# Attention, LayerNorm and feed-forward on one core: four weight halves ahead of the units, an earlier LayerNorm row, and one load for each tail bias tile

## The chip, the core and the metric

The kernel runs on one core of one Trainium2 chip. The metric is the device time of one execution in microseconds (us), taken as the median of the runs shown. Five engines matter: TensorE (PE, with its weight loads as PEld), VectorE (DVE), ScalarE (ACT), GpSimd (POOL) and SyncE (SP). SP and POOL issue nearly all of the DMA transfers.

## What is computed

There are 4 batches of 8 heads, a sequence of 576 and a head width of 64. The feed-forward part goes from 512 to 2048 and back to 512 columns.

```python
scores = scale * np.matmul(q, k.transpose(0, 1, 3, 2))
x = (psi_rel / psi_i)[..., None]
bias = np.maximum(x @ w1 + b1, 0.0) @ w2          # per head, 576 x 576
scores = scores + bias.transpose(2, 0, 1)[None]
attn = softmax(scores)                             # over the last axis
x = matmul(attn, v)                                # heads joined to 512
xn = (x - mean) / np.sqrt(var + 1e-06) * g_ln
out = x + np.maximum(xn @ w_ch1, 0.0) @ w_ch2
```

## The kernel before

**Bias.** The bias is the same for all batches, so it is built once. Its 36 groups of 16 rows go through a small network on ACT, DVE and PE (`bias_relu` L153, `bias_mm` L167). `bias_mm` evicts a group to a staging tile `ev` and writes that by DMA to a DRAM tensor `nb`, of which there is one for each chunk `c` of 128 rows (chunk 4, the tail, has only 64). The first 12 groups are written by POOL's queue, the rest by SP's. The order of the groups begins with the tail chunk: its four groups are needed first.

**Units.** The attention is cut into 144 units (b, c, h), a batch, a chunk of rows and a head; a tail unit (c = 4) holds two heads of 64 rows each. The list `ORD` (L213) sets their order: (0, 4), (1, 4), (1, 0), (0, 0), ... Each unit takes four score matmuls (`qk` L377, written to `sps`), one DVE instruction that adds the bias tile `ldb` and takes the row maximum (L434 in `softmax1`, called "softmax u" below), an exp on ACT (L438), and the product with V (`pv` L496, written to `xps`). The first 24 units keep their probabilities in f32 and are transposed on PE (`ptm` and `ptl`); later ones are cast to f16 and transposed by DMA.

**Bias tiles and other loads.** `issue_loads(u)` (L277) issues the loads of K, Q and V on POOL's queue and those of bias tiles on SP's, as their due times in units come. A tail bias tile is read in two loads of 64 rows (L328, L329).

**Weights.** The two feed-forward matrices arrive as 32 halves of 512 KB, each on SP's queue (`load_w` L610, the load on L627). While `n < 24` a load that is issued inside the loop over units waits for the latest softmax. `decode_w` (L634) turns a half into f32 by three DVE instructions (L643, L646, L648) and feeds a Gram matmul on PE (L657). When the last half of a group (0 to 4, 4 to 8, 8 to 16 of the 16 row blocks) is decoded, `w_scale` (L660) derives the group's scales (`winv`, `wred`), and `split_w` (L677) makes an f16 high part on ACT (L683) and a low part on DVE (L686).

**The loop.** Two halves are loaded and decoded ahead of the loop (L812, L828). Step `u` runs softmax 1 of unit `u`, the loads that are due, two `load_w` calls, and as many decodes as the pace asks for:

```python
if wdec and 32 - len(wdec) < 2 + (4 * max(0, u - 1) + 2) // 3:
```

The row `gs_sb` (LayerNorm's g) is loaded in step 1 behind a wait for the latest softmax (L846); `g_scale` (L692, first instruction L693) reads it in step 3. In step 9, `FILL` (L403) puts 68 matmuls without use (`spin`, L410) on PE. Feed-forward work is cut into micros that fill PE between units: `hps` (L709) is the first product, `y` (L738) the second, with evictions on ACT (L715) and DVE (L719, L749). A scheduler sets the order of instructions on each engine from priorities and dependencies, and each engine executes in that order.

Of the kernel before, what the change touches and what calls it, by code (L numbers as in the profile page):

```python
# [22 lines left out]
def kernel(  # L23
# [14 lines left out]
    NB, NH, SEQ, D = 4, 8, 576, 64  # L38
# [23 lines left out]
    def halves(t):  # L62
# [29 lines left out]
        for c in range(5)  # L92
    ]
    nbias = [
        t[0:(128 if c < 4 else 64) * NH * PITCH].rearrange("(i h j) -> i h j", h=NH, j=PITCH)
        [:, :, 16:16 + SEQ] for c, t in enumerate(nflat)
    ]
    wslot = [wp.tile([128, 1024], F32, name=f"w{f}") for f in range(NF - 1)]
    wend = wp.tile([128, 2048], F32, name="wend")
    wslot += [wend[:, 0:1024], wend[:, 1024:2048]]  # L100
# [37 lines left out]
    def after(ins, dep):  # L138
        if dep is not None:
            tc.add_manual_dep(ins.ins, dep.ins.name,  # L140
                              mybir.DependencyInfo(mybir.DependencyClass.Sync,
                                                   mybir.DependencyReason.DATA),
                              reason="pace")
# [23 lines left out]
    def bias_mm(gi):  # L167
# [40 lines left out]
        dst = nflat[c][r0 * row:(r0 + 16) * row + 16]  # L208
        dst = dst.rearrange("(k x) -> k x", k=16)[:, 0:row]
        dst = dst.rearrange("k (h j) -> k h j", h=NH)[:, :, 0:ntot]  # L210
        (G if gi in gorder[0:12] else SY).dma_start(out=dst, in_=ev[:, 0:ntot])

    ORD = [(0, 4), (1, 4), (1, 0), (0, 0), (2, 0), (3, 0), (3, 4), (2, 4),  # L213
# [20 lines left out]
    uv = {}  # L234
# [29 lines left out]
    for u, (b, c, h) in enumerate(units):  # L264
        key = (seg[vis[u]], c, h)
        buse[key] = buse.get(key, 0) + 1
    vneed = {0: -5, 1: 1, 2: min(uv[2] - 15, ustart[2, 0] - 8),
             3: min(uv[3] - 15, ustart[3, 0] - 8)}
    for b in range(NB):
        for g in range(4):  # L270
# [6 lines left out]
    def issue_loads(u):  # L277
        wait = set()
        for item in list(loads):
# [31 lines left out]
            elif kind == "v":  # L311
                raw = vp.tile([128, 640], F32, tag="v", name="vf")
                ld = G.dma_start(out=raw.rearrange("p (a b c) -> p a b c", a=2, b=5),
                                 in_=v_p[key[0], :, 2 * key[1]:2 * key[1] + 2])
                if ttri:
                    after(ld, ttri[max(ttri)])
                vraw[key] = raw
            else:
                _, c, h = key
                if not bfree[0] or mm_done[0] < gend[c]:  # L320
                    wait.add(kind)
                    continue
                bfree[0] -= 1
                raw = ldp.tile([128, SEQ], F32, tag="ld", name="ldb")
                if c < 4:
                    SY.dma_start(out=raw, in_=nbias[c][:, h, :])
                else:
                    SY.dma_start(out=raw[0:64], in_=nbias[4][:, 2 * h, :])  # L328
                    SY.dma_start(out=raw[64:128], in_=nbias[4][:, 2 * h + 1, :])  # L329
                bt[key] = raw  # L330
            loads.remove(item)

# [476 lines left out]
    wload = [(f, i) for f in range(NF) for i in range(2)]  # L809
    wdec = list(wload)  # L810
    NP = 7
    for _ in range(2):  # L812
        load_w()
    issue_loads(-6)
    issue_loads(-5)
# [5 lines left out]
    for n in range(NP + 1):  # L821
        if n < NP:
            bias_relu(gorder[n], 3)
        if n > 0:
            bias_mm(gorder[n - 1])
            mm_done[0] += 1
    ngroup = NP
    for _ in range(2):  # L828
        decode_w(*wdec.pop(0))

    def flush():
# [6 lines left out]
    def at(step, fn):  # L838
        todo.setdefault(step, []).append(fn)

    for b in range(NB):
        u0 = uv[b]
        for g in range(4):
            at(u0 - 11 + g, lambda b=b, g=g: v_max(b, g))
            at(u0 - 4 + 2 * g if b else u0 - 4 + 2 * g, lambda b=b, g=g: split_v(b, g))
    at(1, lambda: after(SY.dma_start(out=gs_sb, in_=g_r), ttri[max(ttri)]))  # L846
    at(3, g_scale)
    issue_loads(0)
    qk(0)
    qk(1)  # L850
    with tc.high_priority(offset=-40):
# [12 lines left out]
    while u < NU + 6 or jobs or cur_job or pend or yq:  # L864
# [16 lines left out]
            if wload:  # L881
                load_w()
        for _ in range(8):
            if wdec and 32 - len(wdec) < 2 + (4 * max(0, u - 1) + 2) // 3:
                f, i = wdec.pop(0)
                decode_w(f, i)
                if i == 1 and f + 1 == GROUPS[GOF[f]][1]:
                    w_scale(GOF[f])
# [106 lines left out]
```

## Time and profile before

| what | us |
| --- | --- |
| three runs | 678.59, 682.61, 681.12 |
| median | 681.12 |
| span of the profiled execution | 676.2 |
| busy PE / DVE / ACT / POOL in it | 647.0 / 457.6 / 392.0 / 97.3 |

The profiled execution's own time is not listed apart from its span; the span is 4.9 us under the median of the runs (681.12 - 676.2). A busy time is the sum over instructions of one engine. The notation `[2.81 <-DMA gs_sb<-in_g_r_dram]` at a row's end says how long the engine stood idle just before the row, and what ended that. An engine name with a q (SPq) is its sequencer: the time for which it issues a transfer.

### The profile page before, as it was taken

Reading aid. Unit: us, or ns where it says so; the run is one execution under the profiler, and the core shown is the slowest. Engines: PE = TensorE matmul, PEld = TensorE weight load, DVE = VectorE, ACT = ScalarE, POOL = GpSimd, SP = SyncE. Lnnn points to the kernel's source line nnn. Section 1 sums busy time; section 2 is a strip of 40 time slices with the busy share of each in tenths; the row PEclk is TensorE's granted clock in tenths of the full one; section 3 lists DMA queues with packets and bytes.
Section 4 is the critical chain, followed back from the end, with each engine's and each line's share of the span. In section 5 each row is a group of like instructions: output and inputs, shape, how many; then the busy total and the mean of one; then the engine's idle time right before and its main releaser. Section 6 shows DMA issues by size and latency. Waiting matters only on the chain.

```text
span 676.2 us, 19145 instructions
## 1 busy us (share of the span) xinstructions
PE 647.0 (96%) x7929; PEld 448.4 (66%) x7929; DVE 457.6 (68%) x1061; ACT 392.0 (58%) x777; POOL 97.3 (14%) x163
## 2 busy tenths in 40 slices
PE   6789996999999999999899999999999999999997
PEld 4457774676466666666667766666776776677774
DVE  6588999679757577696757575667576675755321
ACT  5565747378958466887755576676554454453110
POOL 5412321011000011111101010111011120000000
PEclk9989997899999999999899999999999999999999
DMA  8999885444668997868769779699997886744100
GB/s 313 295 405 335 298 291 173 143 87 105 136 132 169 227 235 171 176 154 169 174 159 223 156 161 174 151 182 180 184 214 150 160 162 121 128 88 87 33 16 17
DMA packets 187015, 117.24 MB, mean 173 GB/s; under 512 B 164016, under 2 KB 164144, under 8 KB 186928
## 3 DMA queue, kind: packets, MB, share of 16 engines
q1 hardware_dynamic: 177184, 81.00, 54.7%
q0 software_dynamic: 9600, 34.84, 17.0%
q8 instruction: 62, 1.02, 0.6%
q10 hardware_dynamic: 144, 0.18, 0.1%
q14 instruction: 25, 0.20, 0.1%
HBM read 60.51 MB, written 15.63 MB: 113 GB/s over the span
## 4 chain that ended last, share of the span: by engine, by line
PE 50%; DVE 0%; ACT 0%; issue 0%
PE hps L709 19%; PE y L738 18%; PE sps L391 6%; PE xps L480 6%; PE bps L181 1%; DVE v L369 0%; DVE x L749 0%; DVE e L462 0%; ACT e L443 0%; DVE x L516 0%; ACT t L438 0%; DVE e L464 0%
## 5 line engine op out<-in xcount | busy, mean ns | idle before, releaser
L709 PE MATMUL hps<-xT,w 128*128 128x128 f16 x3240 | 197.1, 221 | 2.8 <-DVE w L686 2.1
L738 PE MATMUL y<-w,hh 128*128 128x512 f16 x810 | 189.8, 382 | 2.9 <-ACT hh L715 2.8
L709 PEld LDWEIGHTS <-w 128*128 128x128 f16 x3240 | 185.4, 99 | 8.3 <-DVE w L686 3.6
L438 ACT ACTIVATE t<-t,m 128x576 f32<-128x576 f32 x144 | 110.9, 770 | 135.6 <-DVE m L434 135.2
L738 PEld LDWEIGHTS <-hh 128*128 128x128 f16 x864 | 79.8, 98 | 91.9 <-ACT hh L715 3.9
L462 DVE SCALAR_TENSOR_TENSOR e<-t,e 128x512 f16<-128x512 f32 x120 | 82.8, 690 | 77.1 <-ACT e L443 76.8
L434 DVE CUSTOM_DVE_ANT_0 t<-sps,ldb 128x576 f32<-128x576 f32 x144 | 105.9, 753 | 33.7 <-PE sps L391 20.8
L391 PE MATMUL sps<-kf,qf 64*128 64x288 f32 (+1 forms) x640 | 95.9, 434 | 4.3 <-DVE m L434 4.3
L443 ACT ACTIVATE e<-t 128x576 f16<-128x576 f32 x120 | 80.8, 678 | 4.9 <-DMA wend<-e 2.5
L715 ACT ACTIVATE hh<-hps 128x512 f16<-128x512 f32 x72 | 42.0, 583 | 52.4 <-PE hps L709 46.9
L391 PEld LDWEIGHTS sps<-kf,qf 64*128 64x128 f32 (+1 forms) x640 | 48.0, 175 | 36.6 <-issue 17.5
L719 DVE SCALAR_TENSOR_TENSOR hh<-hps,hh 128x512 f16<-128x512 f32 x72 | 49.4, 686 | 33.2 <-ACT hh L715 32.7
L480 PEld LDWEIGHTS <-pt 128*128 128x128 f16 (+1 forms) x1456 | 48.9, 100 | 30.0 <-issue 25.6
L749 DVE SCALAR_TENSOR_TENSOR x<-y,ycs,x 128x512 f32<-128x512 f32 x58 | 43.4, 748 | 34.5 <-PE y L738 34.4
L480 PE MATMUL xps<-v,pt 128*128 128x64 f16 (+1 forms) x1456 | 58.6, 194 | 1.5 <-DMA pt<-e 1.1
L291 POOL DMA_DIRECT2D kf<-in_k_s_dram x56 | 30.8, 551 | 162.0 <-PE sps L391 114.6
L304 POOL DMA_DIRECT2D qf<-in_q_main_dram x32 | 18.4, 576 | 159.8 <-PE xps L480 81.5
L187 ACT ACTIVATE ev<-bps,cb_sb,par_sb 128x144 f32<-128x144 f32 (+27 forms) x48 | 26.0, 592 | 25.8 <-PE bps L181 25.7
L160 ACT ACTIVATE r<-psi_sb,par_sb 128x448 f32<-128x448 f32 (+23 forms) x72 | 39.6, 613 | 0.0
L569 POOL TENSOR_SCALAR rs<-mv 128x1 f32<-128x1 f32 x18 | 9.9, 548 | 146.2 <-DVE mv L568 138.3
L438 ACT ACTIVATION_READ_ACCUMULATOR t<-t,m 128x1 f32 x144 | 27.0, 188 | 0.0
L181 PE MATMUL bps<-r,nw_sb 128*32 128x448 f32 (+24 forms) x200 | 26.9, 494 | 0.0
(121 smaller groups left out, 642.8 us busy)
## 6 DMA issues: line engine op xcount, KB each, us to landing
kf<-in_k_s_dram POOLq DMA_DIRECT2D x56, 288.0 KB, 4.9
w<-in_w_ch_dram SPq DMA_DIRECT2D x22, 512.0 KB, 8.4
ldb<-nb SPq DMA_DIRECT2D x32, 288.0 KB, 4.4
qf<-in_q_main_dram POOLq DMA_DIRECT2D x32, 256.0 KB, 4.7
nb<-ev SPq DMA_DIRECT2D x24, 296.0 KB, 3.3
vf<-in_v_p_dram POOLq DMA_DIRECT2D x16, 320.0 KB, 7.4
wend<-in_w_ch_dram SPq DMA_DIRECT2D x8, 512.0 KB, 4.8
out_dram<-x SPq DMA_DIRECT2D x16, 256.0 KB, 2.3
```

The costliest lines, as they stand in the source:

```text
L160: S.activation(r[:, 0:n], psi_sb[:, 0:n], AF.Relu, bias=pr_sb[:, g4:g4 + 1], scale=1.0)
L391: m = T.matmul(out=o, lhsT=l, rhs=kk, start=True, stop=True, tile_position=(64 * hf, 64 * e))
L434: ttri[u] = V.tensor_tensor_reduce(out=halves(t), in0=ps[:, :, 0:HS], in1=halves(bias), scale=-0.125, scalar=3e38, op0=ALU.add, op1=ALU.mi ...
L438: S.activation(t, t, AF.Exp, bias=m, scale=-1.0, accum_out=l8[b, c][:, h:h + 1])
L443: S.activation(e16[:, 0:SEQ], t, AF.Copy, scale=E_SCALE)
L462: V.scalar_tensor_tensor(out=e16[:, 640:1152], in0=t[:, 0:512], scalar=E_SCALE, in1=e16[:, 0:512], op0=ALU.mult, op1=ALU.subtract)
L480: T.matmul(out=o, lhsT=p[:, m], rhs=v[:, j, a, :], start=(i == 0), stop=(i == len(ops) - 1))
L709: T.matmul(out=h[:, idx * n:idx * n + n], lhsT=w[:, wo + kk * 128:wo + kk * 128 + 128], rhs=xT[k][:, xo + kk, 0:n], start=(i == 0), stop=( ...
L715: S.activation(hh[:, 0], h, AF.Relu)
L719: V.scalar_tensor_tensor(out=hh[:, 1], in0=h, scalar=0.0, in1=hh[:, 0], op0=ALU.max, op1=ALU.subtract)
L738: T.matmul(out=yps[k][t], lhsT=hh[:, a, o:o + 128], rhs=w[:, wo:wo + 512], start=(f == f0 and i == 0), stop=(f == f1 - 1 and i == 2))
L749: V.scalar_tensor_tensor(out=x, in0=y, scalar=ycs[:, g:g + 1], in1=x, op0=ALU.mult, op1=ALU.add)
```

## The change

Five edits. Four halves instead of two are loaded and decoded ahead of the loop, the pace starts from 4, and a half is decoded only if its load has been issued. The load of `gs_sb` stands ahead of the first `qk` and waits for nothing. The V tiles of batch 0 are due from step -3 instead of -5, and `issue_loads(-3)` is called once inside the bias prologue. The tail chunk's `nb` is laid out by head and row, so that a unit's tile is one block of 128 rows, read by one load. Lines after the edits are 3 to 5 higher.

```diff
--- before.py
+++ after.py
@@ -92,9 +92,10 @@
         for c in range(5)
     ]
     nbias = [
-        t[0:(128 if c < 4 else 64) * NH * PITCH].rearrange("(i h j) -> i h j", h=NH, j=PITCH)
-        [:, :, 16:16 + SEQ] for c, t in enumerate(nflat)
+        t[0:128 * NH * PITCH].rearrange("(i h j) -> i h j", h=NH, j=PITCH)[:, :, 16:16 + SEQ]
+        for t in nflat[0:4]
     ]
+    nbias.append(nflat[4][0:64 * NH * PITCH].rearrange("(x j) -> x j", j=PITCH)[:, 16:16 + SEQ])
     wslot = [wp.tile([128, 1024], F32, name=f"w{f}") for f in range(NF - 1)]
     wend = wp.tile([128, 2048], F32, name="wend")
     wslot += [wend[:, 0:1024], wend[:, 1024:2048]]
@@ -208,6 +209,9 @@
         dst = nflat[c][r0 * row:(r0 + 16) * row + 16]
         dst = dst.rearrange("(k x) -> k x", k=16)[:, 0:row]
         dst = dst.rearrange("k (h j) -> k h j", h=NH)[:, :, 0:ntot]
+        if c == 4:
+            dst = nflat[4][r0 * PITCH:r0 * PITCH + 1]
+            dst = bass.AP(dst.tensor, dst.offset, [[PITCH + 1, 16], [64 * PITCH, NH], [1, ntot]])
         (G if gi in gorder[0:12] else SY).dma_start(out=dst, in_=ev[:, 0:ntot])
 
     ORD = [(0, 4), (1, 4), (1, 0), (0, 0), (2, 0), (3, 0), (3, 4), (2, 4),
@@ -264,7 +268,7 @@
     for u, (b, c, h) in enumerate(units):
         key = (seg[vis[u]], c, h)
         buse[key] = buse.get(key, 0) + 1
-    vneed = {0: -5, 1: 1, 2: min(uv[2] - 15, ustart[2, 0] - 8),
+    vneed = {0: -3, 1: 1, 2: min(uv[2] - 15, ustart[2, 0] - 8),
              3: min(uv[3] - 15, ustart[3, 0] - 8)}
     for b in range(NB):
         for g in range(4):
@@ -325,8 +329,7 @@
                 if c < 4:
                     SY.dma_start(out=raw, in_=nbias[c][:, h, :])
                 else:
-                    SY.dma_start(out=raw[0:64], in_=nbias[4][:, 2 * h, :])
-                    SY.dma_start(out=raw[64:128], in_=nbias[4][:, 2 * h + 1, :])
+                    SY.dma_start(out=raw, in_=nbias[4][128 * h:128 * h + 128, :])
                 bt[key] = raw
             loads.remove(item)
 
@@ -809,7 +812,7 @@
     wload = [(f, i) for f in range(NF) for i in range(2)]
     wdec = list(wload)
     NP = 7
-    for _ in range(2):
+    for _ in range(4):
         load_w()
     issue_loads(-6)
     issue_loads(-5)
@@ -824,8 +827,10 @@
         if n > 0:
             bias_mm(gorder[n - 1])
             mm_done[0] += 1
+        if n == 5:
+            issue_loads(-3)
     ngroup = NP
-    for _ in range(2):
+    for _ in range(4):
         decode_w(*wdec.pop(0))
 
     def flush():
@@ -843,9 +848,9 @@
         for g in range(4):
             at(u0 - 11 + g, lambda b=b, g=g: v_max(b, g))
             at(u0 - 4 + 2 * g if b else u0 - 4 + 2 * g, lambda b=b, g=g: split_v(b, g))
-    at(1, lambda: after(SY.dma_start(out=gs_sb, in_=g_r), ttri[max(ttri)]))
     at(3, g_scale)
     issue_loads(0)
+    SY.dma_start(out=gs_sb, in_=g_r)
     qk(0)
     qk(1)
     with tc.high_priority(offset=-40):
@@ -881,7 +886,7 @@
             if wload:
                 load_w()
         for _ in range(8):
-            if wdec and 32 - len(wdec) < 2 + (4 * max(0, u - 1) + 2) // 3:
+            if wdec and wdec[0] in wraw and 32 - len(wdec) < 4 + (4 * max(0, u - 1) + 2) // 3:
                 f, i = wdec.pop(0)
                 decode_w(f, i)
                 if i == 1 and f + 1 == GROUPS[GOF[f]][1]:
```

On SP, at the start of the program, before (the `w` tiles are raw weight halves, `ldb` a bias tile, `nb` its DRAM tensor):

```order
L328 DMA ldb<-nb_128 64x576
L329 DMA ldb<-nb_128 64x576
L627 DMA w_129<-in_w_ch_dram 128x1024
L627 DMA w_132<-in_w_ch_dram 128x1024
L627 DMA w_133<-in_w_ch_dram 128x1024
L627 DMA w_134<-in_w_ch_dram 128x1024
L846 DMA gs_sb<-in_g_r_dram 128x512
L627 DMA w_135<-in_w_ch_dram 128x1024
```

The change, from the first weight load on:

```order
L630 DMA w_129<-in_w_ch_dram 128x1024
L630 DMA w_131<-in_w_ch_dram 128x1024
L630 DMA w_132<-in_w_ch_dram 128x1024
L630 DMA w_133<-in_w_ch_dram 128x1024
L853 DMA gs_sb<-in_g_r_dram 128x512
L332 DMA ldb<-nb_128 128x576 x4
L630 DMA w_129<-in_w_ch_dram 128x1024
L630 DMA w_133<-in_w_ch_dram 128x1024
```

Two weight loads and that of `gs_sb` now stand ahead of the tail bias tiles; a tile is one row instead of two; `gs_sb` no longer stands among the loads that wait for a softmax.

On DVE, around the first softmax (L434 before, L437 now; the row with `m` reads out its maximum), before:

```order
L648 SCALAR_TENSOR_TENSOR w_130<-w_129,w_130 128x512
L648 SCALAR_TENSOR_TENSOR w_130<-w_131,w_130 128x512
L434 ISA t,m<-sps,ldb 128x576
L434 ISA m 128x1
L434 ISA t,m<-sps,ldb 128x576
L434 ISA m 128x1
L162 TENSOR_SCALAR rh<-psi_sb,npr_sb 128x512 x2
L434 ISA t,m<-sps,ldb 128x576
L434 ISA m 128x1
L643 TENSOR_SCALAR w_131<-w_129 128x512
```

The change:

```order
L651 SCALAR_TENSOR_TENSOR w_130<-w_129,w_130 128x512
L651 SCALAR_TENSOR_TENSOR w_130<-w_131,w_130 128x512
L646 TENSOR_SCALAR w_131<-w_132 128x512
L646 TENSOR_SCALAR w_131<-w_133 128x512
L649 SCALAR_TENSOR_TENSOR w_131<-w_132,w_131 128x512
L649 SCALAR_TENSOR_TENSOR w_131<-w_133,w_131 128x512
L651 SCALAR_TENSOR_TENSOR w_131<-w_132,w_131 128x512
L651 SCALAR_TENSOR_TENSOR w_131<-w_133,w_131 128x512
L437 ISA t,m<-sps,ldb 128x576
L437 ISA m 128x1
L437 ISA t,m<-sps,ldb 128x576
L437 ISA m 128x1
```

The six instructions that decode halves 2 and 3 have moved from behind the third softmax to ahead of the first.

On DVE again, around softmax 21 (the `ISA` row; L686, now L689, are the low parts of the splits of weight group 1), before:

```order
L686 SCALAR_TENSOR_TENSOR w_134<-w_135,ws,w_134 128x512
L369 SCALAR_TENSOR_TENSOR v<-vf,vs,v 128x10x64
L646 SCALAR_TENSOR_TENSOR w_142<-w_143,w_142 128x512
L577 SCALAR_TENSOR_TENSOR u<-x,mv,gs_sb 128x512
L434 ISA t,m<-sps,ldb 128x576
L434 ISA m 128x1
L686 SCALAR_TENSOR_TENSOR w_134<-w_135,ws,w_134 128x512
L686 SCALAR_TENSOR_TENSOR w_135<-w_136,ws,w_135 128x512
L648 SCALAR_TENSOR_TENSOR w_142<-w_143,w_142 128x512
L369 SCALAR_TENSOR_TENSOR v<-vf,vs,v 128x10x64
L599 SCALAR_TENSOR_TENSOR x_1639<-u,rs,x_1639 128x512
```

The change:

```order
L689 SCALAR_TENSOR_TENSOR w_135<-w_136,ws,w_135 128x512
L649 SCALAR_TENSOR_TENSOR w_143<-wend,w_143 128x512
L689 SCALAR_TENSOR_TENSOR w_136<-w_137,ws,w_136 128x512
L651 SCALAR_TENSOR_TENSOR w_143<-wend,w_143 128x512
L105 TENSOR_SCALAR vs<-var 128x4
L571 BN_AGGR mv<-bs 128x2
L651 SCALAR_TENSOR_TENSOR w_143<-wend,w_143 128x512
L689 SCALAR_TENSOR_TENSOR w_136<-w_137,ws,w_136 128x512
L359 TENSOR_SCALAR c_1472<-vs 128x8
L580 SCALAR_TENSOR_TENSOR u<-x,mv,gs_sb 128x512
L437 ISA t,m<-sps,ldb 128x576
L437 ISA m 128x1
```

All eight splits of group 1 now stand ahead of softmax 21; before, three did, four stood between softmax 21 and softmax 22, and the last behind softmax 22. On POOL's queue the first K, Q and V loads stand in the order that they had.

## Rows read from the trace of the kernel before

**Rows 1.** Page: busy time of PE, and its busy tenths in 40 slices.

```profile
PE 647.0 (96%) x7929; PEld 448.4 (66%) x7929; DVE 457.6 (68%) x1061; ACT 392.0 (58%) x777; POOL 97.3 (14%) x163
...
PE   6789996999999999999899999999999999999997
```

**Rows 2.** Page: the chain that ended last, by line of the kernel.

```profile
PE hps L709 19%; PE y L738 18%; PE sps L391 6%; PE xps L480 6%; PE bps L181 1%; DVE v L369 0%; DVE x L749 0%; DVE e L462 0%; ACT e L443 0%; DVE x L516 0%; ACT t L438 0%; DVE e L464 0%
```

**Rows 3.** Windows of 15 us: window and length, busy us (instructions) by engine, clock, DMA, GB/s.

```profile
90.00:105.00 15.00, 15.00 (x158) 12.07 (x158) 14.86 (x37) 6.76 (x15) 3.21 (x6) 1.00 0.82 286
105.00:120.00 15.00, 8.46 (x62) 4.96 (x60) 15.00 (x31) 10.96 (x20) 2.76 (x4) 0.68 0.35 98
120.00:135.00 15.00, 14.65 (x95) 10.25 (x96) 9.92 (x23) 5.28 (x14) 0.54 (x1) 0.86 0.50 161
...
150.00:165.00 15.00, 13.44 (x168) 8.56 (x169) 14.00 (x30) 13.17 (x24) 3.24 (x5) 1.00 0.37 81
165.00:180.00 15.00, 14.08 (x138) 8.39 (x138) 13.00 (x27) 15.00 (x29) 0.11 (x1) 1.00 0.62 125
```

**Rows 4.** Timeline of DVE, 20 to 68 us: start, busy us, instruction, idle time before it.

```profile
23.36 0.76 DVE L434 CUSTOM_DVE_ANT_0 t<-sps,ldb 128x576 f32<-128x576 f32 x1 [2.74 <-DMA ldb<-nb]
...
27.24 0.76 DVE L434 CUSTOM_DVE_ANT_0 t<-sps,ldb 128x576 f32<-128x576 f32 x1 [3.12 <-PE bps L201]
...
31.05 0.43 DVE L643 TENSOR_SCALAR w<-w 128x512 uint32<-128x512 uint32 x1 [1.43 <-DMA w<-in_w_ch_dram]
...
40.16 0.69 DVE L693 TENSOR_REDUCE gmax<-gs_sb 128x1 f32<-128x512 f32 x1 [2.81 <-DMA gs_sb<-in_g_r_dram]
...
58.95 0.16 DVE L668 TENSOR_SCALAR wred<-gram 128x2 f32<-128x2 f32 x1 [2.24 <-PE gram L132]
...
67.58 0.76 DVE L434 CUSTOM_DVE_ANT_0 t<-sps,ldb 128x576 f32<-128x576 f32 x1
```

**Rows 5.** Groups by line on DVE: the decoding instructions, busy us and mean ns.

```profile
L646 DVE SCALAR_TENSOR_TENSOR w<-w,w 128x512 uint32<-128x512 uint32 x22 | 14.8, 685 | 0.1
...
L643 DVE TENSOR_SCALAR w<-w 128x512 uint32<-128x512 uint32 x22 | 9.0, 423 | 1.5 <-DMA w<-in_w_ch_dram 1.4
```

**Rows 6.** Windows of 2 us early on, same columns as Rows 3.

```profile
4.00:6.00 2.00, 0.28 (x8) 0.20 (x8) 1.48 (x5) 1.46 (x2) 1.78 (x4) 1.00 1.01 416
...
16.00:18.00 2.00, 1.93 (x41) 1.24 (x32) 2.00 (x6) 1.89 (x3) 0.81 (x2) 1.00 0.65 182
```

**Rows 7.** Transfers issued by SP up to 62 us: count, KB each, median us to landing.

```profile
w<-in_w_ch_dram SPq DMA_DIRECT2D x15, 512.0 KB, 7.8
...
ldb<-nb SPq DMA_DIRECT2D x9, 144.0 KB, 5.9
...
gs_sb<-in_g_r_dram SPq DMA_DIRECT2D x1, 256.0 KB, 11.1
```

**Rows 8.** Timeline of SP's sequencer, 18 to 30 us.

```profile
18.52 0.55 SPq L328 DMA_DIRECT2D ldb<-nb  x1
...
24.15 4.86 SPq L627 DMA_DIRECT2D w<-in_w_ch_dram  x4
```

**Rows 9.** Timeline of PE, 68 us: the first scores behind the spins.

```profile
68.40 0.76 PE L391 MATMUL sps<-kf,qf 64*128 64x288 f32 x4 [0.62 <-DVE m L434]
```

**Rows 10.** Timeline of DVE: softmax 21 and the last split of group 1.

```profile
109.80 0.74 DVE L434 CUSTOM_DVE_ANT_0 t<-sps,ldb 128x576 f32<-128x576 f32 x1
...
118.54 0.74 DVE L686 SCALAR_TENSOR_TENSOR w<-w,ws,w 128x512 f16<-128x512 f32 x1
```

**Rows 11.** Timeline of PE, 116 to 125 us.

```profile
116.00 0.73 PE L709 MATMUL hps<-xT,w 128*128 128x128 f16 x10 [2.15 <-DVE w L686]
...
118.77 1.03 PE L738 MATMUL y<-w,hh 128*128 128x512 f16 x2 [1.35 <-ACT hh L715]
...
121.35 3.72 PE L738 MATMUL y<-w,hh 128*128 128x512 f16 x10
```

**Rows 12.** The chain of waits late in the program: start, us, and twelve `y` matmuls.

```profile
528.80 2.59 PE y L738 x12
```

## The prediction

> **What bounds the kernel now.** I read the page first. PE is busy 96% of the span, and in the 40 slices its digit is 9 nearly everywhere but in the first three, in slice 7, in slice 20 and in the last [rows 1]. The chain that ended last is feed-forward and attention matmuls, with the lines of DVE and ACT at 0% each [rows 2]. So the late part is PE back to back, and a change in loads and weight decoding can only act where PE is not full: before about 185 us. Next I read windows of 15 us over that stretch [rows 3]. Between 105 and 120 us PE works 8.46 of 15 us, DVE all 15.00: there DVE is the bound, and the granted clock is 0.68, so that part of the stretch ran at the lower of PE's two levels (1.2 and 2.4 GHz). From 150 to 180 us ACT is nearly full (13.17 and 15.00 of 15). What DVE does at 105 us it could not do before, so the third view is DVE's own timeline, for idle time ahead of that. From 19 to 59 us it stands idle five times at length: 2.74 us ahead of softmax 0, 3.12 ahead of softmax 1, 1.43 for the third weight half, 2.81 for `gs_sb`, 2.24 for a matmul of the scales of group 0 [rows 4]. These make 12.3 us. From 90 to 120 us DVE is busy 29.86 of 30 us [rows 3]. So the argument is: an idle microsecond of DVE that is filled early is one less of DVE work in the stretch where PE waits for it.
>
> **The two extra halves.** A half costs DVE three instructions, 423, 685 and about 685 ns [rows 5], 1.8 us, so two cost 3.6. They move, they are not added: all 32 halves are decoded in both. They now stand behind the second half's decode, which ends at 20.6 us (23.36 less the 2.74 of idle time), and ahead of softmax 0, that is, in the first hole. With them DVE is ready for softmax 0 at about 24.1, against 23.36 now. If the bias tile still lands when it does, the first hole is gone and softmax 0 is 0.8 us later.
>
> **What the earlier loads cost.** Two halves and `gs_sb` are 1.31 MB more in front of the K, Q, V loads and the writes of the tail bias. Between 4 and 6 us the DMA engines move 416 GB/s at a share of 1.01; between 16 and 18 us 182 GB/s at 0.65 [rows 6]. At 416 GB/s the 1.31 MB last 3.2 us. The slack of the second window is (416 - 182) GB/s times 2 us, 0.47 MB or 1.1 us, and there is more next to it. So softmax 0 is held up by something between nothing and 3.2 us: between 24.1 and 26.5 us. I take 24.8, because the weight halves are needed only at 20 us while the slack lies ahead of that; 0.7 us of the first hole stays. The rule that speaks against this edit is that of the Trainium skill, page "DMA: Bandwidth & Descriptors", section "Issuing engines are not separate DMA queues": transfers that different engines start run on the same 16 DMA engines and interleave. By that rule the whole 3.2 us would fall on POOL's transfers, and the sum below would be the second rival's; the trace agrees in so far as the share is already 1.01 with both queues at work.
>
> **One load for a tail tile.** SP issued the eight half tiles from 18.52 us on, 0.55 us for the first [rows 8], some 4.4 us in all; four whole ones take 2.2 us. The tile of unit 1 is then issued at about 19.1 and, with a landing of 5.9 us as of the half tiles [rows 7], is there at about 25.0, when softmax 0 is just done. The second hole goes from 3.12 to nothing, but unit 2 then waits some 0.7 us for its scores, since PE was not ahead there; I keep 0.7, bounds 0 and 3.1. The four tail tiles later in the program save 2.2 us of SP's time, which no row waits for: nothing. The write to `nb` has as many pieces of the same size: nothing.
>
> **The fifth half.** Its load waits for softmax 0, as that of the third half did. That one was issued 0.8 us behind softmax 0 [rows 4, 8] and its data came about 7 us later. With softmax 0 at 24.8 the fifth half is there at 25.6 plus 6.8, or plus the median of 7.8 [rows 7], at 32.4 to 33.4; DVE has by then done softmax 2 and what follows and stands there at about 30.1. The hole of 1.43 becomes 2.2 to 3.3; I take 2.8. The waiting instruction holds the units behind it too, as it did before. The condition that a half's load must have been issued only moves a decode in the order.
>
> **`gs_sb` and the scales.** The row is issued about 28 us earlier, needs at most its landing time of 11.1 us [rows 7], and is there long before step 3: 2.81 goes to nothing. The scales of group 0 come a unit earlier, with decodes beside them; the hole of 2.24 is between 0 and 2.24 and I take 1.2. The V tiles of batch 0 stand on POOL's queue where they stood: nothing.
>
> **The sum.** Of 12.3 us of holes 0.7 + 0.7 + 2.8 + 1.2 = 5.4 stay, so DVE gains 6.9. By the order, and with each instruction at its group's mean, the work on DVE ahead of softmax 8 is 49.9 us, against 46.8 before: softmax 8 comes at 67.58 [rows 4] + 3.1 - 6.9 = 63.8, and 3.1 us of later decoding are done by then. The 68 spins and the scores behind them, which waited for DVE [rows 9], follow 3.8 us earlier. Until softmax 21 the work ahead of it is 96.5 us against 90.2, with all splits of group 1 in it; the last one of these came at 118.54 [rows 10]. It moves from behind about 119 us of the timeline to about 106 to 108, so `hps` does not wait the 2.15 us that stand ahead of it at 116, nor `y` the 1.35 [rows 11]. Where DVE is the bound, its 6.9 us pass on whole.
> To this comes the clock. Ten `y` took 3.72 us at 121 us [rows 11], while twelve take 2.59 late in the program [rows 12], 2.16 for ten. A full clock in the two windows from 105 to 135 would be worth (1 - 0.68) x 8.46 + (1 - 0.86) x 14.65 = 4.8 us at most, nothing at least; I take half, 2.4, since PE is not idle so often but still idle. Against it, from 150 to 180 us ACT sets the pace; PE stands idle 1.56 + 0.92 = 2.5 us there [rows 3], and with PE earlier it waits more: between 0 and 2.5, I take 1.4. The sum is -6.9 - 2.4 + 1.4 = -7.9 us. The profiled execution has a span of 676.2, so 668.3 after; the median of the runs is 4.9 above that span, and I add it: **673.2 us**.
>
> **The rivals.**
> *PE is full anyway (0.17).* From 68.40 us on, behind a wait of 0.62, PE works, and in the window from 90 to 105 it is at 15.00 of 15 [rows 3, 9]. If the stretch behind does not shorten, because the same splits and decodes meet the same units a little earlier, what is left is the earlier arrival, 3.8 us: 677.3. For it: the DVE work between softmax 20 and 21 grows. Against it: PE's idle time at 116 to 119 has splits and evictions behind it as its releasers.
> *The loads collide (0.18).* The 3.2 us fall on the bias writes whole. Softmax 0 comes at 26.5, the holes that stay are 2.4 + 0.7 + 2.8 + 1.2 = 7.1, DVE gains 5.2, the clock half of what I took: -5.2 - 1.2 + 1.4 = -5.0, or 676.1. For it: the share of 1.01. It decides from a softmax 0 beyond about 25.5.
> *The pile ahead of softmax 21 (0.13), slower.* Between softmax 20 and 21 DVE has 15.4 us of work instead of 10.9, and all of it is executed in order. The units behind have nothing to give PE meanwhile. PE stands idle 4.5 us more, a further stretch like that from 105 to 120 at the lower clock costs 2.7, and the 3.3 us of work that now stand ahead of softmax 31 fall into the window in which ACT and DVE are nearly full. With the 3.8 of earlier arrival: 4.5 + 2.7 + 3.3 - 3.8 = +6.7, or 687.8. It decides if softmax 21 comes later than 112, against 109.80 now [rows 10]. Against it: the feed-forward work of group 0, and of group 1 as soon as its splits are done, lies ready for PE.
> *The change doesn't do what it says (0.10).* The wait for the third half is replaced by a like wait for the fifth and the holes ahead of softmax 0 and 1 come back in other places; only the 2.81 of `gs_sb` remain: 678.3.
>
> **How the numbers follow.** The forecast has 0.42. A measurement of this kernel can tell about 0.5%, 3.4 us, from no change: below 677.7 is faster, above 684.5 slower. Faster is the forecast, most of the second rival (0.15) and half of the first (0.09): 0.66. Same is the rest of these and most of the last: 0.20. Slower is the third and a remnant: 0.14. The lower end has every hole but that of the fifth half (2.2) closed and the clock full, 10.1 + 4.8 = 14.9 less: 666.2, which I round to 666.5. The upper end takes in all rivals but the third: 681.0.
>
> **What would show it.** Right: softmax 0 at 24 to 25.5, no idle time ahead of the maximum of `gs_sb`, a hole of 2 to 3.5 us ahead of the fifth half, softmax 8 at about 63.8, the last split of group 1 by 108, PE over 10 of 15 us between 105 and 120. Wrong: softmax 0 beyond 25.5 (loads collide); softmax 8 early but PE's idle time moved and as long (PE full); softmax 21 beyond 112 (pile); a hole of 5 us or more anywhere before 60 us.

## The result, and the profile after

The changed kernel takes 670.23 us, the median of 4 runs (669.15 to 672.57), against 679.86 (677.76 to 682.61) for the kernel before: a ratio of 0.9863, with a 95% interval of 0.9827 to 0.9899. The forecast was 673.2. On another occasion (e5 below) the ratio was 0.9848 (0.9801 to 0.9895). Some runs of a kernel are over 1.5% slower than its fastest, mostly at a lower granted clock: ratios leave these out, the medians given here do not.

The span of the profiled execution is 668.3 us, against 676.2. That is 7.9 less, which is what the sum of the prediction came to; how much of that is luck is said further down. The execution itself took 670.07, so 1.8 us lie around its span; the prediction had added 4.9, the distance of the old span from the old median, and that is why its time is 3 us too long.

First the windows of 15 us of the changed kernel, with the columns of [rows 3]:

```profile
90.00:105.00 15.00, 13.28 (x120) 10.00 (x120) 13.77 (x33) 7.47 (x14) 1.75 (x4) 0.88 0.68 249
105.00:120.00 15.00, 13.38 (x104) 10.07 (x103) 13.04 (x26) 8.76 (x20) 2.92 (x4) 0.89 0.58 124
120.00:135.00 15.00, 14.36 (x139) 11.80 (x139) 12.38 (x35) 11.28 (x27) 2.37 (x4) 1.00 0.43 118
...
150.00:165.00 15.00, 12.82 (x164) 8.08 (x160) 13.44 (x28) 14.47 (x27) 2.80 (x4) 1.00 0.55 118
165.00:180.00 15.00, 15.00 (x146) 7.90 (x145) 9.31 (x22) 10.00 (x20) 0.00 (x0) 1.00 0.55 102
```

PE is busy 13.38 of 15 us between 105 and 120, where it was 8.46, and the granted clock there is 0.89 instead of 0.68. The window before it has become worse: 13.28 at a clock of 0.88, where it was 15.00. DVE is no longer full in either. So a low clock and idle time have moved ahead and have shrunk.

The same can be had for the whole span, by adding up windows of 2 us: PE's idle time is their length less PE's busy time, and the clock's loss is busy time times (1 - granted clock). What is left is PE's work at full clock.

| stretch, us | idle before | idle after | clock's loss before | clock's loss after |
| --- | --- | --- | --- | --- |
| 0 to 60 | 12.2 | 12.0 | 1.6 | 0.0 |
| 60 to 105 | 1.1 | 2.0 | 0.0 | 2.0 |
| 105 to 135 | 6.5 | 2.3 | 5.3 | 1.2 |
| 135 to 185 | 2.5 | 3.0 | 0.0 | 0.0 |
| from 185 | 6.8 | 8.4 | 1.7 | 0.0 |
| sum | 29.2 | 27.7 | 8.6 | 3.1 |

The work left is 638.5 and 637.4. Of 7.9 us the clock's loss makes 5.5 and idle time 1.5, and 8.3 of all of it is in the stretch from 105 to 135. PE's idle time ahead of 60 us, where the prediction closes holes of DVE, is the same as before (12.0 against 12.2).

Now DVE's timeline, with the rows that answer to [rows 4] (softmax is on L437 in the changed file, decoding begins on L646):

```profile
26.47 0.76 DVE L437 CUSTOM_DVE_ANT_0 t<-sps,ldb 128x576 f32<-128x576 f32 x1 [2.66 <-DMA ldb<-nb]
...
29.91 0.76 DVE L437 CUSTOM_DVE_ANT_0 t<-sps,ldb 128x576 f32<-128x576 f32 x1 [0.48 <-PE sps L394]
...
31.11 0.43 DVE L646 TENSOR_SCALAR w<-w 128x512 uint32<-128x512 uint32 x1 [0.43 <-DMA w<-in_w_ch_dram]
...
33.22 0.43 DVE L646 TENSOR_SCALAR w<-w 128x512 uint32<-128x512 uint32 x1 [0.95 <-DMA w<-in_w_ch_dram]
...
36.86 0.67 DVE L696 TENSOR_REDUCE gmax<-gs_sb 128x1 f32<-128x512 f32 x1
...
54.61 0.14 DVE L671 TENSOR_SCALAR wred<-gram 128x2 f32<-128x2 f32 x1
...
64.25 0.76 DVE L437 CUSTOM_DVE_ANT_0 t<-sps,ldb 128x576 f32<-128x576 f32 x1
```

Softmax 0 comes at 26.47 and not at 23.36, with 2.66 us of idle time still ahead of it, although 3.5 us of decoding have been put in. Softmax 1 follows without a gap, softmax 2 waits 0.48 us for its scores, the fifth and sixth halves 0.43 and 0.95. The maximum of `gs_sb` at 36.86 and `wred` at 54.61 wait for nothing, though the load of `gs_sb` took 14.0 us to land, more than the 11.1 that the prediction called the most. All idle time between the decoding and softmax 8 that a row of the timeline names (2.66, 0.58, 0.48, 0.43, 0.95, 0.75, 0.30, 0.21 and 0.35) is 6.7 us, against 12.5 before. Softmax 8 is 3.3 us earlier.

Why softmax 0 is late is in the transfers that POOL issued in the first 20 us: count, KB each, and the median us from issue to landing. The kernel before:

```profile
nb<-ev POOLq DMA_DIRECT2D x6, 296.0 KB, 3.5
vf<-in_v_p_dram POOLq DMA_DIRECT2D x4, 320.0 KB, 7.4
```

The changed kernel:

```profile
nb<-ev POOLq DMA_DIRECT2D x6, 296.0 KB, 7.7
vf<-in_v_p_dram POOLq DMA_DIRECT2D x4, 320.0 KB, 11.8
```

The writes of the bias and the V tiles take over 4 us longer to land. SP's own queue shows what follows from it:

```profile
22.53 2.56 SPq L332 DMA_DIRECT2D ldb<-nb  x4
27.26 9.90 SPq L630 DMA_DIRECT2D w<-in_w_ch_dram  x8
```

The tail tiles are issued at 22.53, not 18.52 [rows 8], as their writes have landed only then (the first four took a median of 8.5 us, before 3.4). This agrees with the rule that the prediction took from the Trainium skill, page "DMA: Bandwidth & Descriptors", section "Issuing engines are not separate DMA queues".

### The profile page after: what moved, and what is told of

It reads as the page before. It is cut to its first block, busy times and chain, and to the rows that moved or that the text cites. A ratio compares the mean times of both kernels' runs of the same rounds, so it can differ in the third digit from the quotient of the medians.

```text
span 668.3 us, 19124 instructions
## 1 busy us (share of the span) xinstructions
PE 640.6 (96%) x7929; PEld 447.0 (67%) x7929; DVE 456.5 (68%) x1061; ACT 391.5 (59%) x777; POOL 95.7 (14%) x163
## 5 line engine op out<-in xcount | busy, mean ns | idle before, releaser
L741 PE MATMUL y<-w,hh 128*128 128x512 f16 x810 | 187.7, 379 | 3.6 <-DVE x L752 1.6
L437 DVE CUSTOM_DVE_ANT_0 t<-sps,ldb 128x576 f32<-128x576 f32 x144 | 105.7, 752 | 30.7 <-PE sps L394 18.1
L483 PEld LDWEIGHTS <-pt 128*128 128x128 f16 (+1 forms) x1456 | 48.6, 100 | 29.2 <-issue 24.1
```

Of the source, the lines that this page charges most:

```text
L437: ttri[u] = V.tensor_tensor_reduce(out=halves(t), in0=ps[:, :, 0:HS], in1=halves(bias), scale=-0.125, scalar=3e38, op0=ALU.add, op1=ALU.mi ...
L483: T.matmul(out=o, lhsT=p[:, m], rhs=v[:, j, a, :], start=(i == 0), stop=(i == len(ops) - 1))
L741: T.matmul(out=yps[k][t], lhsT=hh[:, a, o:o + 128], rhs=w[:, wo:wo + 512], start=(f == f0 and i == 0), stop=(f == f1 - 1 and i == 2))
```

## The experiments

The comparisons with the kernel before are each with its runs beside them on the same chip; e1 to e4, e5 to e8 and e9 to e12 were run together, and the kernel before had medians of 682.07, 684.16 and 681.11 us there. In the edits, `...` marks what is left out. The edits are against the changed kernel unless said otherwise. Theory A is the prediction's: DVE's early idle time is what counts, and its parts add up. The rivals are named where they came up. The landmark "softmax 36" is used in a table at the end.

**e1: `gs_sb` late again.**

```diff
+    at(1, lambda: after(SY.dma_start(out=gs_sb, in_=g_r), ttri[max(ttri)]))
     at(3, g_scale)
     issue_loads(0)
-    SY.dma_start(out=gs_sb, in_=g_r)
```

> The change, but gs_sb is loaded where it was before (step 1, behind a softmax and the weight loads). Theory A (DVE's early idle time is what counts): a hole of 2 to 3 us ahead of gmax comes back, softmax 8 is 2 to 3 us later than in the changed kernel (64.3), the time is 2 to 3 us longer, about 672.7. Theory B (what counts is that the splits of group 1 stand ahead of softmax 21, which they do here too): softmax 8 is later, but the time stays within 1 us of 670.2.

Measured: 675.79 us, ratio 0.9896 (0.9834 to 0.9957). The hole is back, in DVE's timeline of this kernel:

```profile
41.74 0.69 DVE L696 TENSOR_REDUCE gmax<-gs_sb 128x1 f32<-128x512 f32 x1 [3.55 <-DMA gs_sb<-in_g_r_dram]
```

Softmax 8 comes at 66.93, 2.7 us later than in the change, as A says. By the ratios the time is 3.3 us longer than the change has in e5 (0.9896 against 0.9848, times 682), with intervals that overlap, so that the size of this loss is not settled. The profiled execution, which was the slowest of the six, shows something else. Two windows of it, columns as above:

```profile
66.00:77.00 11.00, 9.05 (x77) 6.38 (x75) 10.91 (x25) 4.88 (x13) 3.29 (x5) 1.00 0.82 266
77.50:101.50 24.00, 24.00 (x114) 19.31 (x113) 21.33 (x53) 13.46 (x33) 4.61 (x8) 0.50 0.79 284
```

PE was busy 9.05 of 11 us from 66 to 77, then the granted clock is 0.50, the lower of the two levels, for 24 us in which PE has no idle time at all. By the reckoning above (busy time times 1 - 0.50) that is 12 us; the work left in this execution comes out at 631.1, not 637.4 as in the change, so the reckoning says too much here, by some 6 us over the whole span. The profiled execution took 681.48, and another run of the same kernel, in the same order, took 669.14 at a mean clock of 0.985 and not 0.966: as short as the change's own runs. Neither A nor B gives such numbers; the clock became a theory of its own (C in e5).

**e2: two halves ahead.**

```diff
-    for _ in range(4):
+    for _ in range(2):
         load_w()
...
-    for _ in range(4):
+    for _ in range(2):
         decode_w(*wdec.pop(0))
...
-            if wdec and wdec[0] in wraw and 32 - len(wdec) < 4 + (4 * max(0, u - 1) + 2) // 3:
+            if wdec and 32 - len(wdec) < 2 + (4 * max(0, u - 1) + 2) // 3:
```

> The change, but with two halves ahead and the old pace; gs_sb early and one load a tail tile are kept. Theory A: the loads no longer collide, so softmax 0 is at about 23.4, but the hole ahead of it stays 2.7 and DVE has two decodes more to do before the units that PE waits for: 1.5 to 3.5 us longer, about 672.7. Rival (the four halves carry nearly all of the gain): 5 us longer or more, 675 to 679. Rival (they carry nothing, since their loads hold softmax 0 up by 3.1 us): within 1 us of 670.2.

Measured: 680.26 us, ratio 0.9997 (0.9961 to 1.0033): the whole gain is gone. DVE's timeline of this kernel:

```profile
22.57 0.76 DVE L437 CUSTOM_DVE_ANT_0 t<-sps,ldb 128x576 f32<-128x576 f32 x1 [2.49 <-DMA ldb<-nb]
...
25.35 0.76 DVE L437 CUSTOM_DVE_ANT_0 t<-sps,ldb 128x576 f32<-128x576 f32 x1 [2.01 <-DMA ldb<-nb]
...
30.36 0.43 DVE L646 TENSOR_SCALAR w<-w 128x512 uint32<-128x512 uint32 x1 [2.55 <-DMA w<-in_w_ch_dram]
33.81 0.43 DVE L646 TENSOR_SCALAR w<-w 128x512 uint32<-128x512 uint32 x1 [3.02 <-DMA w<-in_w_ch_dram]
```

Without the extra loads softmax 0 is at 22.57, with `gs_sb` early: it is the two halves that held it up, not `gs_sb`. But the wait comes back elsewhere: two holes of 2.55 and 3.02 us ahead of the third and fourth halves. Softmax 8 is at 66.17. At that point it looked like the rival by which the four halves carry nearly everything; e6 speaks against that.

**e3: two loads for a tail tile.** The old layout and L328, L329 of the kernel before.

```diff
-                    SY.dma_start(out=raw, in_=nbias[4][128 * h:128 * h + 128, :])
+                    SY.dma_start(out=raw[0:64], in_=nbias[4][:, 2 * h, :])
+                    SY.dma_start(out=raw[64:128], in_=nbias[4][:, 2 * h + 1, :])
...
```

> The change, but each tail bias tile is read by two loads of 64 rows from the old layout. Theory A: softmax 1 waits for its second half tile again, a hole of 1 to 3 us ahead of it; the time is 1 to 2.5 us longer, about 672. Rival (the tile load is hidden behind the scores of unit 2 and the fifth half): within 0.7 us of 670.2.

Measured: 680.23 us, ratio 0.9951 (0.9913 to 0.9989), by the ratios 7.0 us longer than e5. The price that A named isn't there. Softmax 0 and 1 in DVE's timeline:

```profile
26.68 0.76 DVE L434 CUSTOM_DVE_ANT_0 t<-sps,ldb 128x576 f32<-128x576 f32 x1 [2.84 <-DMA ldb<-nb]
...
27.78 0.76 DVE L434 CUSTOM_DVE_ANT_0 t<-sps,ldb 128x576 f32<-128x576 f32 x1 [0.34 <-DMA ldb<-nb]
```

The wait of softmax 1 for its tile is 0.34 us, not 1 to 3; both tiles had to wait for their writes anyway. Yet the time is much longer. A loss without the wait that was to cause it speaks against A's way of adding parts. PE stands idle 28.8 us in its profiled execution, 1.1 more than in the change; what is larger is the clock's loss, 13.5 against 3.1.

**e4: V loads behind the tail writes.**

```diff
-                if ttri:
-                    after(ld, ttri[max(ttri)])
+                after(ld, ttri[max(ttri)] if ttri else evi[gorder[3]])
```

> The change, with the four V loads of batch 0 made to wait for the fourth tail group's eviction, so that they stand behind the four writes of the tail bias on POOL's queue. Theory A with collision as the cost: 1.3 MB less is under way ahead of those writes, they land in 4 us instead of 7.7, softmax 0 is at 24 to 25 instead of 26.5, and the time is 1 to 2 us shorter, about 668.7. Rival (softmax 0 is not what the rest waits for): softmax 0 earlier, the time within 0.7 us of 670.2.

Measured: 675.42 us, ratio 0.9908 (0.9862 to 0.9955). The writes gained, though less than expected: the six landed in a median of 5.3 us, the four of the tail in 4.8, and the tiles were issued at 18.31. But these then took 9.6 us to land, where they take 4.0 in the change: the V loads, issued from 15.46 on, are now under way beside them. So the first softmax still came at 25.70, behind a wait of 5.64, and softmax 8 at 67.57. That the V loads hold the tiles up was not tried by itself. The clock's low stretch of 24 us is here too, with PE busy all of the time, as in e1:

```profile
78.00:102.00 24.00, 24.00 (x113) 19.01 (x112) 21.41 (x53) 13.54 (x33) 4.88 (x8) 0.50 0.79 282
```

PE's idle time is 23.7 us in all, 4.0 less than in the change, and the clock's loss 18.5. Here too there are runs as short as the change's (670.19 at 0.985), and the interval overlaps that of e5.

**e5: the change again, e6: four halves alone.** e6 is the kernel before with the three edits of e2 in the other direction.

> The changed kernel as it is, beside the kernel before on the chip of this call. Theory A (work and waits): ratio 0.986 again, at whatever clock. Theory C (the granted clock makes most of the difference, and that comes by chance): where the mean clock of its runs is no higher than that of before, the ratio is 0.993 to 0.997.

> The kernel before with four halves loaded and decoded ahead and the new pace, nothing else. With two halves and all other edits the gain was gone, so if the halves are the cause: ratio 0.986 to 0.990. Theory A with each hole counted: the holes of gs_sb (2.8) and of softmax 1 stay, ratio about 0.993. If the parts only work together: 0.996 to 1.003.

Measured: e5 672.16 us, ratio 0.9848 (0.9801 to 0.9895). Beside e6 to e8 it holds its gain, at mean clocks of 0.990 to 0.997 for its six runs, where the seventeen of the kernel before have 0.978 to 0.992. The condition of theory C, a clock no higher than before, was not met; but that the clock is higher again speaks against its part by which it comes by chance, whatever the kernel.
e6: 684.06 us, ratio 1.0012 (0.9973 to 1.0051). Four halves alone show no gain, two halves with the rest show none: neither carries it without the other. Softmax 8 is at 67.33. In e6 a row of PE's timeline shows a wait that the changed kernel hasn't:

```profile
127.81 0.61 PE L657 MATMUL gram<-wend 128*128 128x128 bf16 x4 [2.96 <-DVE wend L648]
```

The Gram matmul of a late half stands at that place of PE's order and waits 2.96 us for a decode that waits for its data, and what stands behind it waits too. In the changed kernel DVE waits for that half as well, but PE has transposes and products to do in that time, and its longest wait there is 0.48. A row of DVE and one of PE in the changed kernel:

```profile
122.01 0.43 DVE L646 TENSOR_SCALAR wend<-wend 128x512 uint32<-128x512 uint32 x1 [3.88 <-DMA wend<-in_w_ch_dram]
...
121.36 0.66 PE L459 MATMUL ptm<-par_sb,t 128*128 128x128 f32 x4 [0.48 <-ACT pt L461]
```

**e7: halves 2 and 3 issued later, e8: the V edit undone.** In e7 the two extra `load_w` calls stand behind the first `bias_mm`, and each load waits for its eviction.

```diff
+            elif n in (2, 3):
+                after(ld, evi[gorder[0]])
...
+        if n == 1:
+            load_w()
+            load_w()
```

> The change, with the loads of halves 2 and 3 waiting for the first tail group's eviction at about 10 us, so that K and Q land ahead of them. If the collision with the K, Q, V loads costs: softmax 0 at 25 to 25.5 rather than 26.5 and 0.5 to 1.5 us less than the change. If all of it must pass before 23 us anyway: softmax 0 at 26 to 27, the time within 0.7 us of the change.

> The change with the V tiles of batch 0 due at step -5 as before and without the extra call. POOL's queue has the same order of loads, and PE's order differs only in a few small places. Theory A: no difference, within 1 us of the change on the same chip. Rival (small shifts of the order on PE decide the clock): a difference of 2 us or more, with a different mean clock.

Measured: e8 671.17 us, ratio 0.9853 (0.9804 to 0.9903): no difference. The expectation was wrong in one thing: with the V edit undone the instructions stand in the same order on all five engines, PE too, so there was nothing that could differ. In this kernel the edit does nothing.
e7: 668.24 us, ratio 0.9815 (0.9762 to 0.9868), the shortest median of all; its interval overlaps that of e5, so that it is faster than the change isn't shown. Softmax 0 is at 26.38, as the rival by which all of the data must pass before it anyway had it.
What e5, e7 and e8 have in common is that PE, DVE, ACT and POOL execute one and the same order; only issue times of loads differ. Every variant up to here whose ratio is worse (e1 to e4, e6) had another order, up to about unit 33; of these e1 and e4 are not told apart from e5. That is the ground of theory D: the order that the scheduler gives to the middle units decides.

**e9: more work early, e10: loads later, with the order kept.** In e9 the first decode instruction of the sixth half is issued seven times, in e10 the two extra `load_w` calls stand behind the fourth `bias_mm` and their loads wait for the fourth write of the tail bias.

```diff
+            for _ in range(7 if (f, i) == (2, 1) else 1):
                 dec = V.tensor_scalar(out=w, in0=raw[:, :, 1], scalar1=3, scalar2=0x3FFFFFFF,
...
```

```diff
+            elif n in (2, 3):
+                after(ld, nbw[gorder[3]])
```

> The change with the first decode instruction of the sixth half issued seven times instead of once: 6 x 0.42 = 2.5 us more on DVE between softmax 2 and 8. From softmax 9 on every engine has the changed kernel's order. Every edit undone by itself has cost 4 to 12 us and has also reshuffled the orders up to about unit 33. Theory C (what counts is how early softmax 8 is, and PE's clock multiplies it): softmax 8 at 66 to 67, the time 6 us or more longer, about 678. Theory D (the order that the scheduler gives the middle units decides): at most the 2.5 us, 671 to 674.

> The change with the loads of halves 2 and 3 waiting until the fourth write of the tail bias has landed (18 to 19 us); the order from softmax 9 on is that of the change. Softmax 0 and what follows is later by the landing of these halves, softmax 8 by 1 to 3 us. Theory C: 677 or more. Theory D: as much longer as softmax 8 is later, 671.5 to 674.5.

Measured: e9 672.48 us, ratio 0.9884 (0.9842 to 0.9926). The added work fell mostly into waits that were there: behind softmax 2 DVE's waits up to softmax 8 come to 3.0 us in the change and to 0.4 here. Softmax 8 moved by 0.4 us; by the ratios the time is 2.5 us longer than e5, with intervals that overlap. It says little more than that such work is hidden.
e10: 682.09 us, ratio 1.0039 (1.0002 to 1.0077). By its number this looks like C. Its timeline tells otherwise:

```profile
24.16 0.43 DVE L650 TENSOR_SCALAR w<-w 128x512 uint32<-128x512 uint32 x1 [3.73 <-DMA w<-in_w_ch_dram]
...
44.95 0.43 DVE L650 TENSOR_SCALAR w<-w 128x512 uint32<-128x512 uint32 x1 [5.20 <-DMA w<-in_w_ch_dram]
...
74.31 0.76 DVE L438 CUSTOM_DVE_ANT_0 t<-sps,ldb 128x576 f32<-128x576 f32 x1
```

The expectation of 1 to 3 us was wrong: there is a hole of 5.20 us for a weight half at 45 us besides, and softmax 8 is at 74.31, 10.1 us later than in the change. Softmax 36 is 8.5 us later than in the change, the span 11.4 longer (679.7), the median 9.9 above e5, by the ratios 13. With the order kept from softmax 9 on, a delay of softmax 8 passes on about one to one; nothing multiplies it by two or three, as C, in the form that it has for e9 and e10, would need for the variants before. That fits D and doesn't fit C. It is one kernel, with a delay three times that of any other.

**e11: halves 2 and 3 behind the tail's evictions, e12: `gs_sb` alone.** e11 is e7 with `gorder[3]` for `gorder[0]` and the two `load_w` calls behind the fourth `bias_mm`; e12 is the kernel before with the early load of `gs_sb` only.

> As e7, but the loads of halves 2 and 3 wait for the eviction of the fourth tail group (about 15 us), with the changed kernel's order on PE, DVE, ACT and POOL throughout. If the K, Q, V loads and the bias writes gain by the free DMA engines: the four tail writes land in 4 to 5 us, not 7.7; softmax 0 between 25 and 27, the time 668 to 671. Rival: the halves come too late for DVE, softmax 0 at 28, and 2 us more than the change.

> The kernel before with gs_sb loaded early and nothing else. Theory A (holes of DVE add up): the hole of 2.8 us is gone, softmax 8 at about 65, ratio 0.996 to 0.997. Theory D: softmax 8 at about 65 too, but the ratio is set by the order that comes out, so it need not follow: anything from 0.985 to 1.01, with PE's idle time and low clock between 60 and 140 us to match.

Measured: e11 670.06 us, ratio 0.9863 (0.9815 to 0.9912), with softmax 0 at 27.43 and softmax 8 at 65.30: like the change. The four tail writes landed in a median of 4.7 us, as expected, but softmax 0 came between the two values that were expected for it: DVE waits 2.13 for a half and then 1.13 for its tile. e12: 682.62 us, ratio 0.9971 (0.993 to 1.0012): not told apart from no gain. Softmax 0 is at 22.67, as in e2. Its hole of 2.81 is gone, but a hole of 3.85 stands ahead of the third half, where 1.43 was, and softmax 8 is at 66.92, not at 65.

**All of them by two landmarks.** The start of softmax 8 and of softmax 36 on DVE (us in the profiled execution), how the stretch between them compares with the kernel before, PE's idle time and the clock's loss in that stretch by windows of 2 us as above, and the ratio to the kernel before:

| kernel | softmax 8 | softmax 36 | stretch, against before | PE's idle time in it | clock's loss in it | ratio |
| --- | --- | --- | --- | --- | --- | --- |
| before | 67.58 | 203.43 | 0 | 10.1 | 5.1 | 1 |
| the change | 64.25 | 194.31 | -5.8 | 7.3 | 3.1 | 0.9863 |
| e5 | 64.50 | 193.97 | -6.4 | 7.9 | 1.6 | 0.9848 |
| e7 | 64.28 | 194.05 | -6.1 | 7.9 | 1.5 | 0.9815 |
| e8 | 63.42 | 194.73 | -4.5 | 8.3 | 2.9 | 0.9853 |
| e9 | 64.69 | 195.03 | -5.5 | 8.5 | 3.2 | 0.9884 |
| e11 | 65.30 | 195.93 | -5.2 | 7.6 | 3.2 | 0.9863 |
| e10 | 74.31 | 202.79 | -7.4 | 7.7 | 1.7 | 1.0039 |
| e1 | 66.93 | 202.52 | -0.3 | 5.0 | 17.1 | 0.9896 |
| e2 | 66.17 | 201.28 | -0.7 | 12.5 | 7.7 | 0.9997 |
| e3 | 66.78 | 203.41 | +0.8 | 6.5 | 11.4 | 0.9951 |
| e4 | 67.57 | 203.24 | -0.2 | 5.8 | 17.1 | 0.9908 |
| e6 | 67.33 | 205.76 | +2.6 | 10.4 | 7.7 | 1.0012 |
| e12 | 66.92 | 202.71 | -0.1 | 11.1 | 3.7 | 0.9971 |

The rows fall into two sets. With the changed kernel's order in the middle units the stretch is 4.5 to 7.4 us shorter, whenever it begins. With any other order that came out of a part of the edits it is between 0.7 us shorter and 2.6 longer. With different orders PE may have done more or less feed-forward work by softmax 36, so single differences of a microsecond mean nothing there; the gap between the two sets does.

What parts the sets is the clock: its loss is 1.5 to 3.2 us in the first and 3.7 to 17.1 in the second. PE's idle time doesn't part them. In e2, e6 and e12 it is larger than in the change, in e1, e3 and e4 smaller, and there, by this reckoning, the low clock alone makes the stretch longer. Each row is one execution, and the clock is not fixed by the order: over their runs the six kernels with the changed order (without e10) have mean clocks of 0.987 to 0.997, the six with another order 0.961 to 0.992, and the short runs of e1 and e4 are as fast as the change. So what the executions show is that the changed order goes with a higher clock; that the order brings the clock about was not tried by itself.

## Why the prediction came out right

Faster was right, the time is in the range, and the sum of 7.9 us is the one measured between the spans. That it agrees to the tenth is luck, as its terms don't agree. By its steps:

- **The early holes.** Forecast: 12.3 us of idle time fall to 5.4. Measured: 12.5 to 6.7, and softmax 8 at 64.25 where 63.8 was forecast. The size was nearly right, its parts were not. The first hole was to shrink to 0.7 and kept 2.66: the loads did collide, and softmax 0 at 26.47 is the upper bound of 26.5, at which the second rival had placed it. By the prediction's own sign (beyond 25.5) that rival had this step right; its 676.1 us didn't come, since other holes closed further and the clock gave more than both had reckoned. The fifth half was to wait 2.8 and waited 0.43, the sixth 0.95: its load was issued from 27.26 us on and the data was there at 31.11, in 3.9 us and not 7. The scales of group 0 were to keep 1.2 and keep 0.30 (ahead of `winv`). The hole of `gs_sb` is gone, and the second hole with it, with 1.06 ahead of softmax 2 for the 0.7 that was kept; the V edit does nothing, as forecast. So DVE gained 5.8 us, not 6.9.
- **DVE's gain passes on.** The prediction took DVE as the bound at 105 us, so that 6.9 us would pass on whole. In e10 a shift of softmax 8 does pass on about one to one with the order kept. But the 3.1 us of decoding done ahead are not seen as a gain by themselves: softmax 21 came at 110.61, later than before (109.80), as the third rival had it, though short of its 112.
- **The splits.** The last split of group 1 was to come by 108 and came at 109.20. Rows of DVE in the changed kernel:

```profile
109.20 0.74 DVE L689 SCALAR_TENSOR_TENSOR w<-w,ws,w 128x512 f16<-128x512 f32 x1
...
110.61 0.74 DVE L437 CUSTOM_DVE_ANT_0 t<-sps,ldb 128x576 f32<-128x576 f32 x1
...
116.58 0.75 DVE L437 CUSTOM_DVE_ANT_0 t<-sps,ldb 128x576 f32<-128x576 f32 x1
```

  and of PE:

```profile
103.21 2.93 PE L712 MATMUL hps<-xT,w 128*128 128x128 f16 x26
...
107.64 1.74 PE L712 MATMUL hps<-xT,w 128*128 128x128 f16 x22
...
112.95 2.32 PE L741 MATMUL y<-w,hh 128*128 128x512 f16 x10
```

  The waits of [rows 11] at 116 and 118 are gone: the two pieces of `hps` of group 1, 26 and 22, run without a wait for a split, and ten `y` take 2.32 us, not 3.72. PE gains from softmax 22 (0.7 us late) to softmax 24 (8.1 us early), in 9 us of the timeline. The pile at softmax 21 doesn't cost: PE's longest wait between 110 and 120 us is 0.74.
- **The clock.** Forecast 2.4 us, half of a bound of 4.8 from two windows. Measured: a loss of 8.6 falls to 3.1, so 5.5 in all: 4.1 between 105 and 135, where the term was sized, 2.0 given back ahead of that, and 3.3 before 60 us and after 185, where the prediction had nothing. As what the clock gives over the span, the term was too small by more than half; as what it gives from 60 to 135 us (2.1) it was nearly right.
- **What ACT takes back.** Forecast 1.4 between 150 and 180. The lead was 7.85 at softmax 30, 5.97 at 32, 9.12 at 36 and 7.77 at the last softmax: in the end 1.3 from its highest, near the forecast's size. But between 135 and 185 us PE's idle time is only 0.5 larger (3.0 against 2.5), so this term was too large. Behind softmax 36 PE's idle time is 1.6 larger (8.4 against 6.8) and the clock's loss 1.7 smaller (0.0 against 1.7), while the work left is 1.3 larger (465.6 against 464.3): what is given back there is work that had not been done by softmax 36.

So the mechanism was half of the truth. Worked out from the landmarks: 3.3 us are the earlier arrival of softmax 8, which theory A explains. Another 5.8 come between softmax 8 and 36, where PE's idle time is 2.8 smaller, the clock's loss 2.0 and the work left 1.0; and 1.3 are given back. In that stretch the changed kernel has another order of splits, decodes, Gram matmuls and feed-forward work, and all kernels that kept this order have a like stretch. The prediction had looked at two places of that order and reckoned 3.1 us of decoding and 2.4 of clock for it. It had not reckoned with an order that depends on all edits together. Undone one by one, and priced by the difference of the ratio from that of e5 times 682 us, `gs_sb` costs 3.3 (not told apart from nothing), the halves 10.2, one load a tail tile 7.0. That adds up to 20.5, twice the 10.4 that the change gains by the same reckoning, and the last two alone are 17.2, while the halves alone or `gs_sb` alone give no gain that can be told from none. So a price found in this way is not that of the edit alone: the order and the clock changed with it.

What stays open: whether the order brings the higher clock about, and which difference of the order is the one that matters. That e6's Gram matmul waits 2.96 us where the change has none is one such place; that it makes the difference was not tried by itself. Nor was an order held fixed while `gs_sb` or the tail tile was undone.

## What to carry to other kernels

Where a scheduler sets the order, an edit has two effects: the waits that it moves, and the new order that it brings about. Undoing one part measures both; compare the orders first, and to price a wait, move it by a dependence that leaves the order as it is (as in e7, e10 and e11).
Add up the waits on the engine that bounds a stretch and look at the clock of the other one in the same windows; here the clock made 5.5 of the 7.9 us and PE's idle time 1.5. And compare the granted clocks of all runs of a variant before calling its loss a wait: e1 and e4 have runs as short as the change's.

## What the runs showed of the hardware

- A granted clock of 0.50 lasted 24.0 us in e1 (77.5 to 101.5) and in e4 (78 to 102), with PE busy all of the time; ahead of it PE had been busy 9.05 of 11 and 9.21 of 12 us. In the kernel before the low stretches are 7.0 and 6.5 us (from 107 and from 117.5), with 5.3 and 5.1 us busy in them.
- The mean granted clock of one kernel differs from run to run, and its time with it: e1 ran in 669.14 us at 0.985, in 675.53 at 0.972. In the changed kernel a low stretch of 6.5 us stands as well (101.5 to 108).
- 1.3 MB more in flight in the first microseconds raised the landing of a bias write from 3.5 to 7.7 us and that of a V tile from 7.4 to 11.8, but of a K tile only from 6.6 to 8.2. These are medians.
